# Batch 0 of an attention kernel: q and k transposed in quarters of 64 tokens by 64 channels

## The chip, the cores and the metric

The kernel runs on one core of a Trainium2 chip. The core has five engines with one instruction queue each: TensorE (PE in the profile, its weight loads PEld), VectorE (DVE), ScalarE (ACT), GpSimd (POOL) and SyncE (SP). Each engine works through its own queue in order, and waits at an instruction until the semaphores that it names have been raised. The metric is the device time of one execution in microseconds (us). Three executions of the kernel before took 171.11, 171.31 and 171.92 us; the median is 171.31 us.

## The reference

Four batches of eight attention heads, 768 tokens, 64 channels per head. A query sees itself and the 95 tokens before it, and the first 8 tokens of the sequence; the score gets a bias that falls with distance, by a slope of its own for each head. Then a second block works on the result x (768 tokens by 512 channels per batch).

```
scores = scale * q @ k.T + bias          # bias = -slope[h] * distance
a      = softmax(where(keep, scores, -1e9))
x      = a @ v                           # heads side by side: 768 x 512
theta  = x @ w_theta
y      = w_tok_r @ (x*cos(theta)) + w_tok_i @ (x*sin(theta))
u      = x + y
out    = u + relu(u @ w_ch)
```

## The kernel before

A token block is 128 tokens, so there are six blocks. Two heads are always worked together (h0 and h0+1): head h0 on partitions 0 to 63 of the transposed tiles, head h0+1 on partitions 64 to 127.

**Layout of q and k.** `load_qk` (L70) puts token 6p+t on partition p in column group t. The scores need q and k with channels on the partitions, so `att_transpose` (L209) turns them on TensorE into PSUM tiles of the pool `ps_tr` (two buffers), and copies bring them to one SBUF tile `qk`: its first 768 columns are `kT`, the next 768 `qT`, both with tokens in their natural order. Tokens of the first 64 partitions are tokens 0 to 383, tokens of the other 64 partitions are 384 to 767.

For batch 0 (L238 to L250) the function makes two PSUM tiles, `pq` and `pk`. It transposes 12 pieces of q (six column groups, two heads; 128 tokens by 64 channels each), then 12 of k. ScalarE then copies `pk` to `kT` and VectorE copies `pq` to `qT`; each copy takes 768 columns, or two cuts of 258 and 510 columns in the first call (`cuts=(43, T)`). For batches 1 to 3 (L216 to L237) it makes the two PSUM tiles `halves` by partition half instead: `halves[0]` holds k and q of tokens 0 to 383, `halves[1]` those of tokens 384 to 767. It takes 48 transposes of 64 tokens by 64 channels, and each of the two copies takes 768 columns that hold one half of kT and one half of qT.

**After the transposes.** `att_extras` (L254) copies kT's blocks 1 to 4 to a tile part `mT` (L257) and overwrites the first 8 tokens of each block there with the global tokens (L258); it does so on GpSimd, in the first call of batch 0 on VectorE. `prepare_v` (L91, L92) does the like for v. `att_scores` (L279) forms three groups of score blocks: group 0 works on kT alone, groups 1 and 2 need mT as well. In batch 0, groups 0 and 2 get their bias in PSUM from a matmul (`att_bias`, L276) and one exponential (L302); group 1 goes through an exponential (L306) and a multiplication with a table on VectorE (L319). `att_values` (L346) multiplies with v, `att_norm` (L362, L364) divides by the row sums on VectorE, and `turn_x` (L378, L383) transposes x for the next block.

**Order.** The whole order is written out by hand: `K` keeps every instruction in program order on its engine. Batch 0 runs ahead of everything else (L533 to L581):

```
    for h0 in (2, 4, 6):
        att_scores(0, h0, 0)
        att_scores(0, h0, 1, mul=False)
        att_values(0, h0 - 2, apart=True)
        att_norm(0, h0 - 2)
        att_norm(0, h0 - 1)
        if h0 < 6:
            att_transpose(0, h0 + 2)
            ...
        att_mul(0, h0, 1)
        att_scores(0, h0, 2)
```

So on TensorE the values of one pair of heads stand behind the group-1 scores of the next pair, and the transposes of the pair after stand behind those values; on VectorE the copy of a transposed half stands behind the four instructions of the two norms. In batches 1 to 3 the attention of one batch is interleaved with the second block of the batch before (`attend_beside`, L503). `keep_warm` (L133) puts matmuls on zeros into the TensorE queue, whose result nobody reads. The loads of batch 0's later heads, of the weights (`load_wtok`, L104) and of batch 1 stand in GpSimd's queue, between the copies of `att_extras` and `prepare_v`.

Of the kernel before, what the change touches and what calls it, by code (L numbers as in the profile page):

```python
# [16 lines left out]
def kernel(  # L17
# [13 lines left out]
    nc = tc.nc  # L31
    B, H, S, D = q.shape
    T = 128
    NT = S // T
# [19 lines left out]
    K = tc.keep_in_program_order  # L54
# [4 lines left out]
    def ps_acc():  # L59
        return psum.tile([T, DM], FP, name="ps_mm", tag="ps_mm", bufs=2)  # L60

    def ps_tr(cols):
        return psum.tile([T, cols], BF, name="ps_tr", tag="ps_tr", bufs=2)
# [4 lines left out]
    q_sb, k_sb, x_sb = {}, {}, {}  # L68
# [19 lines left out]
    def prepare_v(b, h0, eng=nc.gpsimd):  # L88
        hs = slice(h0, h0 + 2)
        vs, vp = v_sb[b % 2], v_pv[b % 2]  # L90
        K(eng.tensor_copy(out=vp[:, hs, :, :], in_=vs[:, hs, 1:NT - 1, :]))  # L91
        K(eng.tensor_copy(  # L92
            out=vp[0:NG, hs, :, :],
            in_=vs[0:NG, hs, 0:1, :].to_broadcast([NG, 2, NT - 2, D + 1])))
# [38 lines left out]
    def keep_warm(n, tile=None):  # L133

        junk = ps_acc() if tile is None else tile
        for _ in range(n):
            K(nc.tensor.matmul(junk, lhsT=zero[:, 0:T], rhs=zero, start=True, stop=True))
# [13 lines left out]
    ident = const.tile([T, T], BF)  # L151
# [54 lines left out]
    exps, probs, values = {}, {}, {}  # L206
    xTs, zris, css = {}, {}, {}

    def att_transpose(b, h0, extras=True, sins=None, q_eng="dve", between=None, cuts=(T,)):  # L209

        qk = abuf.tile([T, 2 * S + (NT - 2) * T], BF, name="qk", bufs=2)
        kT, qT = qk[:, 0:S], qk[:, S:2 * S]
        qTs[b, h0], kTs[b, h0] = qT, kT
        mTs[b, h0] = qk[:, 2 * S:]
        copy = nc.scalar.copy if q_eng == "act" else nc.vector.tensor_copy
        if b > 0:  # L216

            HP = T // 2
            halves = [ps_tr(S), ps_tr(S)]
            for t_ in range(NT):  # L220
                for i_, src in enumerate((k_sb[b], q_sb[b])):
                    c = (i_ * NT + t_) * HP
                    for r in range(2):
                        P = slice(r * HP, (r + 1) * HP)
                        for hh in range(2):
                            K(nc.tensor.transpose(  # L226
                                halves[r][hh * D:(hh + 1) * D, c:c + HP],
                                src[P, h0 + hh, t_ * D:(t_ + 1) * D], ident[P, P]))
            if sins is not None:
                sins()  # L230
            for r, op in enumerate((nc.scalar.copy, copy)):
                K(op(out=qk[:, 0:2 * S].rearrange("a (i r p t) -> a i r p t",  # L232
                                                  i=2, r=2, t=NT)[:, :, r, :, :],
                     in_=halves[r].rearrange("a (i t p) -> a i p t", i=2, t=NT)))
            if extras:
                att_extras(b, h0)
            return  # L237
        pq, pk = ps_tr(S), ps_tr(S)  # L238
        for src, pst in ((q_sb[b], pq), (k_sb[b], pk)):
            if pst is pk and between is not None:  # L240
                between()
            for t_ in range(NT):
                for hh in range(2):
                    K(nc.tensor.transpose(pst[hh * D:(hh + 1) * D, t_ * T:(t_ + 1) * T],
                                          src[:, h0 + hh, t_ * D:(t_ + 1) * D], ident))

        for op, dst, src in ((nc.scalar.copy, kT, pk), (copy, qT, pq)):
            for p0, p1 in zip((0,) + cuts, cuts):
                K(op(out=dst.rearrange("a (p t) -> a p t", t=NT)[:, p0:p1, :],  # L249
                     in_=src.rearrange("a (t p) -> a p t", t=NT)[:, p0:p1, :]))  # L250
        if extras:
            att_extras(b, h0)

    def att_extras(b, h0, eng=nc.gpsimd, values=True):  # L254
        kT = kTs[b, h0]
        mT = mTs[b, h0]
        K(eng.tensor_copy(out=mT, in_=kT[:, T:S - T]))  # L257
        K(eng.tensor_copy(  # L258
            out=mT.rearrange("a (t p) -> a t p", p=T)[:, :, 0:NG],
            in_=kT[:, None, 0:NG].to_broadcast([T, NT - 2, NG])))  # L260
        if eng is nc.gpsimd and values:
            prepare_v(b, h0)
# [3 lines left out]
    def att_bias(h0, g_):  # L266

        ps = biased[h0, g_] = ps_wide()
        rows = dist.rearrange("a n t -> a (n t)")
        for hh in range(2):  # L270
            if g_ == 0:
                out_, rhs = ps[:, hh, 0:3 * T], rows
            else:
                out_ = ps[:, hh, :].rearrange("a (r x) -> a r x", r=2)
                rhs = rows[:, None, T:3 * T].to_broadcast([T, 2, 2 * T])
            K(nc.tensor.matmul(out_, lhsT=ident_d[:, h0 + hh, :], rhs=rhs,  # L276
                               start=True, stop=False))

    def att_scores(b, h0, g_, mul=True):  # L279
        qT, kT, mT = qTs[b, h0], kTs[b, h0], mTs[b, h0]  # L280
        blocks = GROUPS[g_]
        n = len(blocks)
        bias = b == 0 and g_ != 1
        if bias and (h0, g_) not in biased:
            att_bias(h0, g_)
        ps = biased[h0, g_] if bias else ps_wide()

        runs = [(0, 2)] + [(2, 1)] if g_ == 0 else [(i_, 1) for i_ in range(n)]
        for i_, w in runs:
            it, prev = blocks[i_]  # L290
            if prev == 0 or it == 1:
                keys = kT[:, (it - prev) * T:(it - prev + 1) * T]
            else:
                keys = mT[:, (it - 2) * T:(it - 1) * T]
            for hh in range(2):
                R = slice(D * hh, D * (hh + 1))
                K(nc.tensor.matmul(ps[:, hh, i_ * T:(i_ + w) * T],  # L297
                                   lhsT=keys[R, :], rhs=qT[R, it * T:(it + w) * T],
                                   start=not bias, stop=not bias or i_ == n - 1))
        if bias:  # L300
            p = abuf.tile([T, 2, 4 * T], BF, name="p", bufs=6)
            K(nc.scalar.activation(p[:, :, 0:n * T], ps[:, :, 0:n * T], AF.Exp, scale=scale))  # L302
            probs[b, h0, g_] = p
            return
        e = abuf.tile([T, 2, 4 * T], BF, name="e", bufs=3)
        K(nc.scalar.activation(e[:, :, 0:n * T], ps[:, :, 0:n * T], AF.Exp, scale=scale))  # L306
        exps[b, h0, g_] = e
        if mul:
            att_mul(b, h0, g_)
# [193 lines left out]
    def attend_beside(b, main, lead, load):  # L503


        def m(n=1):
            for _ in range(n):
                main.pop(0)()

        m(lead)  # L510
        for h0 in range(0, H, 2):
            att_scores(b, h0, 0)
            m(2 if h0 else 1)
            att_scores(b, h0, 1)
            att_scores(b, h0, 2)
            if h0 + 2 < H:
                att_transpose(b, h0 + 2, q_eng="act")
                if load and h0 == 0:
                    load_heads(b + 1, 0, 4)
                if load and h0 + 4 == H:  # L520
                    load_heads(b + 1, 4, 4)
                m(2)
            else:
                if load:
                    turn_x(b, NC - 2, False)
                m(len(main) - 1)
            att_values(b, h0)
            if h0 + 2 < H and not (load and h0 + 4 == H):
                turn_x(b, h0 // 2, True)
        m()  # L530
# [4 lines left out]
    for src, dst in ((first[:, 0], q_sb[0]), (first[:, 1], k_sb[0])):  # L535
        K(nc.vector.tensor_copy(out=dst[:, 0:2, :], in_=src))
    att_bias(0, 0)
    att_transpose(0, 0, extras=False, between=lambda: keep_warm(1), cuts=(43, T))
    make_ident_d(2, 6)
    att_extras(0, 0, nc.vector)  # L540
    prepare_v(0, 0, nc.vector)
    keep_warm(1)
    att_scores(0, 0, 0)
    att_scores(0, 0, 1)
    att_transpose(0, 2, extras=False)
    att_extras(0, 2, nc.gpsimd, False)
    prepare_v(0, 2)
    load_wtok(0)
# [1 line left out]
# [4 lines that stand above are left out]
        att_norm(0, h0 - 2)  # L554
        att_norm(0, h0 - 1)
        if h0 < 6:
            att_transpose(0, h0 + 2)
            if h0 == 2:
                load_wtok(1)
            else:  # L560
                load_heads(1, 0, 4)
# [3 lines that stand above are left out]
            turn_x(0, h0 // 2 - 1, False)  # L565
# [101 lines left out]
```

## Time and profile before

| | |
|---|---|
| profiled execution, own time | 171.33 us |
| its span, first to last instruction | 169.5 us |
| median of three executions | 171.31 us |
| PE busy | 158.7 us (94% of the span), 1965 instructions |
| DVE busy | 114.7 us (68%) |
| ACT busy | 103.0 us (61%) |
| POOL busy | 63.2 us (37%) |
| transposes of batch 0 (L244) | 96, from 5.9 to 18.2 us |
| copies of batch 0 (L249) | 5 on VectorE, 5 on ScalarE, from 6.6 to 19.6 us |
| granted TensorE clock | 1.000 |

Times in the trace count from the start of the span. The busy shares are averages over a kernel with different stages: the first 36 us are batch 0 alone, in which the engines hand work to each other in turn, and after that TensorE has work of two batches at once. What a change in batch 0 is worth must therefore be read in the first 22 us. The chain of waits goes back from the last instruction: at each step it names what released it, or the instruction ahead of it on its engine.

### The profile page before, as it was taken

The numbers are of one execution on the slowest core, as the hardware profiler recorded it, in microseconds if no ns is written. First come the engines' busy times: TensorE is split into PE (matmuls) and PEld (weight loads), VectorE is DVE, ScalarE is ACT, GpSimd is POOL, SyncE is SP. The second block draws the span as 40 slices with busy tenths as digits, with TensorE's granted clock in tenths as the row PEclk, the third lists the DMA queues.
The fourth block names the chain that finished last, engine by engine and source line by source line (L and its number), as shares of the span: only waits on it lengthen the run. The fifth ranks groups of instructions, "written<-read, shape, count | busy, mean of one in ns | idle before, by whom it ended". The sixth has DMA issues, their size and how long they took to land.

```text
span 169.5 us, 4624 instructions
## 1 busy us (share of the span) xinstructions
PE 158.7 (94%) x1965; PEld 86.2 (51%) x1988; DVE 114.7 (68%) x210; ACT 103.0 (61%) x120; POOL 63.2 (37%) x99
## 2 busy tenths in 40 slices
PE   7779999999899999999999999999999999999992
PEld 2346665555465654446555554445655544444440
DVE  7768875965858875767587694849568756534362
ACT  4989887957686562798658615996765618300010
POOL 8996797004484650032972900054245000000000
PEclk9999999999999999999999999999999999999999
DMA  4999999999999999910599999711953342121325
GB/s 148 194 180 190 209 211 208 198 180 182 158 140 196 141 173 215 257 70 4 92 145 170 155 187 197 210 62 37 73 110 95 99 148 86 68 60 34 113 102 186
DMA packets 57060, 24.08 MB, mean 142 GB/s; under 512 B 43088, under 2 KB 54096, under 8 KB 57040
## 3 DMA queue, kind: packets, MB, share of 16 engines
q0 software_dynamic: 35328, 12.45, 65.5%
q1 hardware_dynamic: 21440, 10.95, 31.2%
q10 hardware_dynamic: 272, 0.39, 0.7%
q8 instruction: 15, 0.25, 0.6%
q14 instruction: 5, 0.04, 0.1%
HBM read 25.69 MB, written 6.29 MB: 189 GB/s over the span
## 4 chain that ended last, share of the span: by engine, by line
PE 80%; DVE 6%; DMA 4%; issue 3%; POOL 3%; ACT 3%; DVEq 0%; ACTq 0%; POOLq 0%
PE ps_mm L430 35%; PE ps_mm L472 12%; PE ps_w L395 11%; PE ps_w L297 7%; PE ps_w L346 5%; DMA v_sb<-in_v_dram 4%; PE ps_tr L226 3%; PE ps_mm L346 2%; ACT e L306 2%; PE ps_tr L114 2%; DVE zri L411 1%; DVE w_tokT L117 1%; PE ps_tr L378 1%; DVE p L319 1%; ACT qk L249 1%
## 5 line engine op out<-in xcount | busy, mean ns | idle before, releaser
L430 PE MATMUL ps_mm<-zri,w_tokT 128*128 128x512 bf16 x276 | 67.0, 380 | 1.3 <-issue 0.8
L306 ACT ACTIVATE e<-ps_w 128x1024 bf16<-128x1024 f32 (+1 forms) x40 | 37.1, 958 | 17.8 <-PE ps_w L297 17.8
L430 PEld LDWEIGHTS <-w_tokT 128*128 128x128 bf16 x288 | 26.2, 98 | 30.3 <-issue 2.3
L257 POOL COPY qk<-qk 128x512 bf16<-128x512 bf16 x15 | 9.5, 636 | 65.2 <-ACT qk L232 53.0
L319 DVE TENSOR_TENSOR p<-e,wmask 128x1024 bf16<-128x1024 bf16 x28 | 19.9, 712 | 11.8 <-ACT e L306 11.8
L403 ACT ACTIVATE cs<-ps_w,halfpi 128x1024 bf16<-128x1024 f32 x12 | 13.4, 1116 | 18.6 <-PE ps_w L395 18.6
L435 DVE TENSOR_TENSOR u<-x_sb,ps_mm 128x512 bf16<-128x512 bf16 x24 | 16.2, 683 | 12.2 <-PE ps_mm L430 12.2
L395 PE MATMUL ps_w<-w_theta_bf,xT 128*128 128x512 bf16 x91 | 22.6, 379 | 0.6 <-ACT cs L404 0.3
L411 DVE TENSOR_TENSOR zri<-cs,x_sb 128x1024 bf16<-128x1024 bf16 x24 | 16.1, 688 | 9.1 <-ACT cs L403 7.7
L472 PE MATMUL ps_mm<-w_ch_bf,uTd 128*128 128x512 bf16 x82 | 21.5, 379 | 0.6 <-issue 0.5
L297 PE MATMUL ps_w<-qk 64*128 64x128 bf16 (+1 forms) x320 | 16.1, 223 | 2.3 <-DVE qk L249 0.8
L475 DVE SCALAR_TENSOR_TENSOR o_sb<-ps_mm,u 128x512 f32<-128x512 f32 (+2 forms) x25 | 16.5, 664 | 1.1 <-PE ps_mm L472 0.9
L232 ACT COPY qk<-ps_tr 128x768 bf16<-128x768 bf16 x21 | 16.0, 815 | 2.0 <-issue 2.0
L297 PEld LDWEIGHTS <-qk 64*128 64x128 bf16 x320 | 10.0, 94 | 12.1 <-issue 7.8
L346 PEld LDWEIGHTS <-p 128*128 128x128 bf16 x352 | 13.2, 97 | 4.6 <-DVE p L319 0.8
L395 PEld LDWEIGHTS <-xT 128*128 128x128 bf16 x96 | 9.0, 98 | 10.8 <-issue 0.5
L80 POOL DMA_DIRECT2D v_sb<-in_v_dram x10 | 13.0, 1299 | 0.0
L472 PEld LDWEIGHTS <-uTd 128*128 128x128 bf16 x88 | 8.2, 98 | 9.0 <-issue 0.2
L404 ACT ACTIVATE cs<-ps_w 128x1024 bf16<-128x1024 f32 x12 | 12.2, 1020 | 0.0
L92 POOL COPY v_pv<-v_sb 8x520 bf16<-8x520 bf16 x15 | 11.5, 767 | 0.9
L354 DVE TENSOR_TENSOR x_sb<-ps_w,rec 128x768 bf16<-128x768 f32 x12 | 11.5, 958 | 0.4
L346 PE MATMUL ps_w<-v_sb,p 128*128 128x65 bf16 x168 | 11.3, 193 | 0.0
(84 smaller groups left out, 180.2 us busy)
## 6 DMA issues: line engine op xcount, KB each, us to landing
out_dram<-o_sb SPq DMA_DIRECT2D x23, 256.0 KB, 2.3
q_sb<-in_q_dram POOLq DMA_DIRECT2D x6, 384.0 KB, 6.2
k_sb<-in_k_dram POOLq DMA_DIRECT2D x6, 384.0 KB, 9.0
v_sb<-in_v_dram POOLq DMA_DIRECT2D x6, 384.0 KB, 13.5
w_nat<-in_moe_w_tok_r_dram POOLq DMA_DIRECT2D x1, 1152.0 KB, 12.3
w_nat<-in_moe_w_tok_i_dram POOLq DMA_DIRECT2D x1, 1152.0 KB, 13.4
v_sb<-in_v_dram POOLq DMA_DIRECT2D x4, 192.0 KB, 6.7
q_sb<-in_q_dram POOLq DMA_DIRECT2D x3, 192.0 KB, 5.9
```

Source lines behind the costliest of these rows:

```text
L232: K(op(out=qk[:, 0:2 * S].rearrange("a (i r p t) -> a i r p t", i=2, r=2, t=NT)[:, :, r, :, :], in_=halves[r].rearrange("a (i t p) -> a i ...
L297: K(nc.tensor.matmul(ps[:, hh, i_ * T:(i_ + w) * T], lhsT=keys[R, :], rhs=qT[R, it * T:(it + w) * T], start=not bias, stop=not bias or i_ ...
L306: K(nc.scalar.activation(e[:, :, 0:n * T], ps[:, :, 0:n * T], AF.Exp, scale=scale))
L319: K(nc.vector.tensor_mul(p.rearrange("a h (r x) -> a h r x", r=2), e.rearrange("a h (r x) -> a h r x", r=2), wmask[:, hs, None, T:3 * T].t ...
L346: K(nc.tensor.matmul(dst, lhsT=lhsT, rhs=rhs, start=(i_ == 0), stop=(i_ == len(mms) - 1)))
L395: K(nc.tensor.matmul(pth[:, s2, :], lhsT=xTs[b][:, dc, c:c + T], rhs=w_theta_bf[:, dc, :], start=(dc == 0), stop=(dc == NC - 1)))
L403: K(nc.scalar.activation(cs[:, :, 0, :], pth, AF.Sin, bias=halfpi))
L411: K(nc.vector.tensor_mul(zris[b][:, st:st + 2, wi, :].rearrange("a s (c d) -> a s c d", d=T), cs[:, :, wi, :].rearrange("a s (c d) -> a s ...
L430: K(nc.tensor.matmul(acc, lhsT=w_tokT[wi][:, st, tt * T:(tt + 1) * T], rhs=zris[b][:, st, wi, :], start=(done[b, tt] == 0), stop=(done[b, ...
L435: K(nc.vector.tensor_add(us[b][:, tt, :].rearrange("a (c d) -> a c d", d=T), x_sb[b][:, :, tt, :], acc.rearrange("a (c d) -> a c d", d=T)))
L472: K(nc.tensor.matmul(pc[:, 0:N], lhsT=uT[:, c:c + T], rhs=w_ch_bf[:, dc, cols], start=(dc == 0), stop=(dc == NC - 1)))
L475: K(nc.vector.scalar_tensor_tensor(o_sb, in0=pc[:, 0:N], scalar=0.0, in1=us[b][:, tt, cols], op0=ALU.max, op1=ALU.add))
```

## The change

Batch 0 takes the way of the other batches: two PSUM tiles by partition half, 48 transposes of 64 by 64, and two copies that each hold one half of k and q. The two ways become one function body, and a parameter `engs` names the engine of each of the two copies. In batch 0 VectorE copies the first half of the tokens and ScalarE the second. The first call transposes q before k (with one `keep_warm` matmul in between, as before) and no longer cuts its copies. Its `att_extras` now stands ahead of the six `make_ident_d` instructions on VectorE, and two more `keep_warm` matmuls stand between the group-0 and group-1 scores of the first pair of heads. For batches 1 to 3 the instructions and their order stay as they were; GpSimd's and SyncE's queues hold the same instructions in the same order throughout.

```diff
-    def att_transpose(b, h0, extras=True, sins=None, q_eng="dve", between=None, cuts=(T,)):
+    def att_transpose(b, h0, extras=True, sins=None, engs=("act", "dve"), between=None):
...
-        pq, pk = ps_tr(S), ps_tr(S)
-        for src, pst in ((q_sb[b], pq), (k_sb[b], pk)):
-            if pst is pk and between is not None:
+        HP = T // 2
+        halves = [ps_tr(S), ps_tr(S)]
+        order = [(t_, i_) for t_ in range(NT) for i_ in range(2)]
+        if between is not None:
+            order = [(t_, i_) for i_ in (1, 0) for t_ in range(NT)]
+        for n_, (t_, i_) in enumerate(order):
+            if n_ == NT and between is not None:
                 between()
-            for t_ in range(NT):
+            src = (k_sb[b], q_sb[b])[i_]
+            c = (i_ * NT + t_) * HP
+            for r in range(2):
+                P = slice(r * HP, (r + 1) * HP)
                 for hh in range(2):
-                    K(nc.tensor.transpose(pst[hh * D:(hh + 1) * D, t_ * T:(t_ + 1) * T],
-                                          src[:, h0 + hh, t_ * D:(t_ + 1) * D], ident))
-
-        for op, dst, src in ((nc.scalar.copy, kT, pk), (copy, qT, pq)):
-            for p0, p1 in zip((0,) + cuts, cuts):
-                K(op(out=dst.rearrange("a (p t) -> a p t", t=NT)[:, p0:p1, :],
-                     in_=src.rearrange("a (t p) -> a p t", t=NT)[:, p0:p1, :]))
+                    K(nc.tensor.transpose(halves[r][hh * D:(hh + 1) * D, c:c + HP],
+                                          src[P, h0 + hh, t_ * D:(t_ + 1) * D], ident[P, P]))
+        if sins is not None:
+            sins()
+
+        for r, eng in enumerate(engs):
+            K((nc.scalar.copy if eng == "act" else nc.vector.tensor_copy)(
+                out=qk[:, 0:2 * S].rearrange("a (i r p t) -> a i r p t",
+                                             i=2, r=2, t=NT)[:, :, r, :, :],
+                in_=halves[r].rearrange("a (i t p) -> a i p t", i=2, t=NT)))
...
-                att_transpose(b, h0 + 2, q_eng="act")
+                att_transpose(b, h0 + 2, engs=("act", "act"))
...
-    att_transpose(0, 0, extras=False, between=lambda: keep_warm(1), cuts=(43, T))
+    att_transpose(0, 0, extras=False, engs=("dve", "act"), between=lambda: keep_warm(1))
+    att_extras(0, 0, nc.vector)
     make_ident_d(2, 6)
-    att_extras(0, 0, nc.vector)
     prepare_v(0, 0, nc.vector)
     keep_warm(1)
     att_scores(0, 0, 0)
+    keep_warm(2)
     att_scores(0, 0, 1)
-    att_transpose(0, 2, extras=False)
+    att_transpose(0, 2, extras=False, engs=("dve", "act"))
...
-            att_transpose(0, h0 + 2)
+            att_transpose(0, h0 + 2, engs=("dve", "act"))
```

More of the change, by code (lines that the diff above doesn't have):

```diff
@@ L214, in att_transpose @@
         mTs[b, h0] = qk[:, 2 * S:]
[L215 to L219, printed above, removed]
-            for t_ in range(NT):
[L221 to L237, printed above, removed]
@@ L238, in att_transpose @@
-        pq, pk = ps_tr(S), ps_tr(S)
-        for src, pst in ((q_sb[b], pq), (k_sb[b], pk)):
-            if pst is pk and between is not None:
+        HP = T // 2
[5 more added lines that the diff above has]
+            if n_ == NT and between is not None:
                 between()
-            for t_ in range(NT):
+            src = (k_sb[b], q_sb[b])[i_]
+            c = (i_ * NT + t_) * HP
+            for r in range(2):
+                P = slice(r * HP, (r + 1) * HP)
```

## The prediction

> **What bounds the kernel now.** I read the page's shares first, then the chain of waits over the first 24 us, then the timeline of single engines there.
>
> ```profile
> span 169.5 us, 4624 instructions
> PE 80%; DVE 6%; DMA 4%; issue 3%; POOL 3%; ACT 3%; DVEq 0%; ACTq 0%; POOLq 0%
> ```
>
> TensorE carries 80% of the chain, but nearly all of it after 21 us. The changed lines run before that, where the chain of waits reads (start us, us, what):
>
> ```profile
> 3.03 6.30 DMA v_sb<-in_v_dram
> ...
> 9.35 0.92 DVE v_pv L91
> ...
> 11.18 0.88 DVE qk L249
> 12.06 0.04 issue
> 12.10 0.56 PE ps_w L297 x12
> 12.66 0.78 PE ps_mm L346 x22
> 13.44 0.77 PE ps_tr L244 x23
> 14.21 0.11 issue
> 14.32 0.81 ACT qk L249
> 15.13 0.05 issue
> 15.19 0.62 POOL qk L257
> 15.81 0.05 issue
> 15.86 0.56 POOL qk L258
> ```
>
> It goes on in the same circle: scores and values on PE, transposes, ScalarE's copy of k, GpSimd's two copies to mT, the next group-1 scores at 16.47, and once more until 20.75. Two things are to be seen. Until 9.33 us the kernel waits for the first load of v, which the change does not touch, so nothing gained before that counts. And in the circle it is ScalarE's copy, which now holds all of kT, that releases GpSimd. VectorE's copy of q is not on the chain there. Its timeline shows why that matters:
>
> ```profile
> 13.85 0.18 DVE L362 RECIPROCAL rec<-ps_mm 128x6 f32<-128x6 f32 x1
> 14.07 0.56 DVE L364 TENSOR_TENSOR x_sb<-ps_mm,rec 128x384 bf16<-128x384 f32 x1
> 14.54 0.95 DVE L249 COPY qk<-ps_tr 128x768 bf16<-128x768 bf16 x1
> 15.41 0.93 DVE L319 TENSOR_TENSOR p<-e,wmask 128x1024 bf16<-128x1024 bf16 x1
> ```
>
> The copy of q stands behind the norm of the second head and ends at 15.49, 0.36 us after ScalarE's copy of k (15.13). Nobody minds, since GpSimd needs only kT. After the change each copy holds half of kT, so L257 must wait for both; in the order of the built programs GpSimd's copy waits for ScalarE before, and for VectorE and ScalarE after.
>
> **The change part by part.**
>
> *Transposes.* 24 per call become 48. The same form runs in batches 1 to 3: 48 of them go from 36.45 to 37.03, 0.58 us, against 0.86 us for 24 of the old form (13.37 to 14.23). So they end 0.28 us earlier. In the two calls of the circle this buys nothing, as VectorE's copy starts later than they end (below). The next matmul then follows a gap of 0.16 us (37.03 to 37.19); start to next matmul is 0.74 us against 0.79 (13.37 to 14.16), so no cost.
>
> *Copies.* The new form has rows of its own: 951 to 957 ns on VectorE and 805 ns on ScalarE (L232), against 945 and 797 (L249, uncut). Below 0.02 us a call, taken as 0.
>
> *First call.* Before, the uncut parts start early: VectorE at 6.58, ScalarE at 7.36. After, both copies wait for all 48. The k part starts behind q's and the junk matmul, which was at 6.79; 24 quarters take about 0.19 us of issue and 0.20 of the last one's length, so the copies start at about 7.2 (estimate). Bounds: not before the cast of k ends (6.33) plus 0.39, 6.75, and not after the old end of the k part, 7.36. VectorE then has its copy 0.95, L257 0.30, L258 0.17 (its rows of before), about 0.07 of gaps, and six identity scalings 0.89, in this order: 2.38 us, to 9.57. The v copy L91 starts there instead of at 9.35: +0.2 (bounds 0, if it still waits for v, and +0.4). What follows, L92, L319 and the copy of the second call, moves along. ScalarE does not hold it: scores at 8.2 plus 0.34, exponentials 0.81 and 1.02 end at about 10.4, and L319 would start at 10.7.
>
> *The two extra junk matmuls.* They run at 0.21 us each (four of L430 take 0.86), while PE waited 0.69 us for VectorE's L258. Cost 0. Without that cover they would cost 0.43 us on PE, but the second exponential would still wait for the first (L302, 0.81), so less on the chain.
>
> *Second call (heads 2 and 3).* VectorE's copy ended at 12.06, ScalarE's at 10.97, and GpSimd started at 11.03 in between, so that mT was ready at 11.93, before VectorE's copy. Now mT comes behind it: 12.06 + 0.05 + 0.62 + 0.05 + 0.21 = 12.99, the scores of group 1 start 0.05 later and take 0.40, and the values start at 13.44 instead of 12.66: +0.78. In PE's queue the values, the transposes and the next scores all stand behind that wait.
>
> *Third and fourth call (the circle).* From the end of the values to the end of VectorE's copy it takes 2.05 us (13.44 to 15.49; 17.64 to 19.69), and these are norms and the copy, which the faster transposes do not shorten: they end 0.58 us after the values, the norms 1.19 us. GpSimd starts 0.06 us behind: 2.11 us after the values instead of 1.75 (13.44 to 15.19) and 1.83 (17.64 to 19.47). So +0.36 and +0.28. GpSimd's pair takes 1.23 us from start to end in both (15.19 to 16.42, 19.47 to 20.70), of which L258's 0.55 is long against 0.21 in most rows. I keep 1.23, since the same multiplication L319 runs beside it. Bounds: 0.62 + 0.05 + 0.21 = 0.88, which would take 0.35 off each call, and the multiplication ahead of GpSimd, +0.14 each (worked below).
>
> On that contention the row is L319: 0.93 and 1.02 us beside GpSimd's copies against a median of 0.69, with L258 stretched to 0.55; the two take turns. The Trainium skill, SBUF — State Buffer, section "SBUF: two separate sides", says that the port pair that VectorE and GpSimd share is an exclusive lock held for a whole instruction, and that whoever starts first blocks the other. By these rows the trace agrees, and after the change VectorE would start first; the rival below prices that.
>
> *Moved with it.* GpSimd's loads stand behind its copies and move by 1.0 to 1.6 us. The token weights (L102) go out at 13.12 and 17.60 and take 12.3 and 13.4 us: landed at 25.4 and 31.0, used at 27.67 and 33.08, and their users move by the same amount. Batch 1's q, k and v are used from 36.4 us on. Cost 0; the cover is about 2 us. From 21 us on the chain is PE, VectorE and ScalarE work with no transfer in it, so a delay at 20.75 goes through to the end.
>
> *Sum:* 0.2 + 0.78 + 0.36 + 0.28 = +1.62 us. The profiled execution took 171.33 us (span 169.5 and 1.8 around it), 0.02 above the median. 171.33 + 1.62 = 172.95 us.
>
> **The rivals.**
>
> 1. *The multiplication goes first and GpSimd waits.* In the third and fourth call GpSimd now starts 0.06 us after VectorE's copy ends, and L319 starts at that end or 0.08 us ahead of it, as the rows 14.54 + 0.95 and 15.41 show. Then L257 waits for it: 16.20 + 0.67 = 16.87, + 0.62 + 0.05 + 0.21 = 17.75 instead of 17.61. Twice 0.14: 173.2 us. Against it: L257 in the trace is never above 0.77 us, but it has hardly ever started just behind such an instruction. Still slower.
>
> 2. *GpSimd's pair gets shorter.* If L257 and L258 run undisturbed in 0.88 us, 0.7 us come back: 172.25 us. For it: 13 of 15 L258 take 0.21 us. Against it: both long rows stand beside exactly this multiplication.
>
> 3. *The delay is absorbed (no change).* If some link after 21 us waited in truth for a load that does not move, the 1.62 us would vanish in that wait: 171.3 us. The place would be the first matmuls on w_theta (22.68) or the transposes of the token weights (27.67, 33.08). It decides when such a load lands less than 1.62 us ahead of its use. Against it: w_theta, sent at 10.12 with 9.7 us to landing, is there at 19.8, and the token weights' loads move along with their users.
>
> 4. *VectorE is not late (not slower).* If VectorE were free whenever the transposes end, its copy of the second call would be done before ScalarE's (10.97), which costs nothing, and in the circle GpSimd would be released 0.58 + 0.04 + 0.95 + 0.05 = 1.62 us after the values instead of 1.75 and 1.83: 0.34 us gained, 171.0 us. It decides where the copy of the third call starts, in old times: before 14.19 it gains, behind it loses. The last norm occupies VectorE until 14.63, and VectorE keeps its written order, so the trace speaks against it.
>
> **How the numbers follow.** Main forecast 172.95: 0.58. Rival 1: 0.16. Rival 2: 0.11. Rival 3: 0.09. Rival 4: 0.06, half of it with the shorter pair of rival 2 on top, which makes it 170.3. A difference of 0.5%, 0.86 us, is about what a measurement of this kernel can tell from no change: slower means above 172.17, faster below 170.45. The main case and rival 1 are slower, and rival 2 in 8 parts of 11: slower 0.82. Faster is the half of rival 4: 0.03. Same is the rest: 0.15. The main case's own range has the first call at 0 to 0.4 and half of the contention's bounds: 172.5 to 173.5. The range down to 171.9 takes in rival 2 with the first call at 0 (171.33 + 0.7 = 172.05), and up to 174.0 rival 1 with the first call at 0.4 and one more blocked GpSimd copy (0.34).
>
> **What the profile after will show.** L245 (the old L257) on GpSimd released by VectorE's copy and not ScalarE's, starting near 12.3, 16.5 and 21.1 us. ScalarE's copy done 0.6 us or more before VectorE's. PE idle ahead of the group-1 scores of heads 2, 4 and 6. Transposes of a call within 0.6 us. The first batch-1 transposes near 38.1 instead of 36.45. The forecast is wrong if VectorE's copy starts when the transposes end, if GpSimd starts before it is done, or if the batch-1 transposes start near 36.5.

## The result, and the profile after

The changed kernel is slower. Its median is 173.46 us (172.95 to 173.71, six executions); the kernel before, run beside it, had 171.42 us (171.11 to 171.92, six executions). The ratio is 1.0114, with a 95% interval of 1.0093 to 1.0135: 1.6 to 2.3 us. The ratios here and below are of fast executions alone and can differ by up to 0.2% from the quotient of the medians beside them. The profiled execution took 173.48 us. The page opens:

```profile
span 171.7 us, 4845 instructions
PE 76%; DVE 9%; DMA 7%; issue 2%; POOL 2%; ACT 2%; DVEq 0%; POOLq 0%; ACTq 0%
```

VectorE's part of the chain has gone from 6% to 9%, and DMA's from 4% to 7%. Both are read below. This is the chain of waits over batch 0 in the changed kernel (start us, us, what):

```profile
8.16 0.85 PE ps_mm L137 x2
9.01 0.56 PE ps_w L285 x7
...
9.60 1.03 ACT e L294
...
10.65 0.69 DVE p L307
11.34 0.88 DVE qk L235
...
12.36 0.62 POOL qk L245
...
13.04 0.22 POOL qk L246
...
13.30 0.40 PE ps_w L285 x8
13.70 0.46 PE ps_mm L334 x11
...
15.66 0.88 DVE qk L235
...
16.66 0.94 POOL qk L245
...
17.65 0.22 POOL qk L246
...
17.92 0.40 PE ps_w L285 x8
```

Before, TensorE went on from VectorE's second-call copy straight to the scores at 12.10 and the values at 12.66. GpSimd's two copies of that call started behind ScalarE's copy and were done ahead of VectorE's, as its timeline before shows:

```profile
11.03 0.63 POOL L257 COPY qk<-qk 128x512 bf16<-128x512 bf16 x1
11.72 0.21 POOL L258 COPY qk<-qk 128x32 bf16<-128x32 bf16 x1
```

Now GpSimd's two copies (L245 and L246, the old L257 and L258) stand between VectorE's copy and the group-1 scores: from 12.22 to 13.30. In the circle, ScalarE's copy has left the chain. The norms and VectorE's copy (15.66) have taken its place, and GpSimd starts behind them. The timelines of GpSimd (with the releaser in brackets) and of VectorE, in the changed kernel, say the same:

```profile
12.36 0.61 POOL L245 COPY qk<-qk 128x512 bf16<-128x512 bf16 x1 [1.44 <-DVE qk L235]
16.66 0.94 POOL L245 COPY qk<-qk 128x512 bf16<-128x512 bf16 x1 [1.40 <-DVE qk L235]
```

and on VectorE the multiplication that starts ahead of the second of them:

```profile
16.44 0.68 DVE L307 TENSOR_TENSOR p<-e,wmask 128x1024 bf16<-128x1024 bf16 x1
```

ScalarE's copies end at 11.31, 15.92 and 20.62 in its own timeline, 0.91, 0.62 and 0.54 us before VectorE's (12.22, 16.54, 21.16).

The same instructions in both profiles give the delay step by step:

| instruction | before | after | shift | added by this step |
|---|---|---|---|---|
| first multiplication (VectorE) | 10.51 | 10.65 | +0.14 | 0.14 |
| end of VectorE's second-call copy | 12.06 | 12.22 | +0.16 | 0.02 |
| values of heads 0 and 1 start | 12.66 | 13.70 | +1.04 | 0.88 |
| group-1 scores of heads 4, 5 | 16.47 | 17.92 | +1.45 | 0.41 |
| group-1 scores of heads 6, 7 | 20.75 | 22.54 | +1.79 | 0.34 |
| first transposes of batch 1 | 36.52 | 38.32 | +1.80 | 0.01 |
| TensorE's work from 106 us on | | | +2.18 | 0.38 |

From 27 to 103 us the shift stays at 1.80, so nothing on the way absorbs what batch 0 has lost. The last 0.38 us is not batch 0. In the chain of waits of the changed kernel it stands here:

```profile
96.84 8.33 DMA uTd<-u
...
105.21 1.04 PE ps_mm L460 x4
```

This load transposes a tile of `u`. Before, it went out at 95.05, took 7.7 us and landed at 102.76, only 0.07 us before TensorE began to load it as weights (102.83); TensorE did not wait. Now it takes 8.33 us, and TensorE waits. In the two chains its user starts 2.00 us later than before (105.21 and 103.21), and the four matmuls take 1.04 instead of 0.86 us. With the first load of q and k (4.25 us, now at the head of the chain where the load of v was with 6.30) this 8.33 us makes DMA's 7%.

One more thing differs. The windows view of the changed kernel (stretch, length, busy us of PE, PEld, DVE, ACT, POOL with instruction counts, granted TensorE clock, DMA share, GB/s) reads:

```profile
9.00:10.20 1.20, 1.20 (x57) 1.00 (x56) 1.09 (x4) 0.62 (x2) 1.20 (x3) 0.50 1.60 165
...
12.00:14.00 2.00, 1.29 (x26) 0.71 (x25) 0.21 (x1) 1.85 (x3) 1.51 (x4) 1.00 1.75 186
```

For about 3.4 us, from 8.3 to 11.7, TensorE ran at half its clock; the kernel before ran at 1.00 throughout. The six executions speak against a large price: two had the full clock all through and took 172.95 and 173.66 us, the four with a low stretch 173.42 to 173.71. Still, a second theory had to be tested: that the low clock, not the later link to GpSimd, makes the loss.

### The profile page after: what moved, and what is told of

It reads as the page before. It is cut to its first block, busy times and chain, and to the rows that moved or that the text cites. A ratio compares the mean times of both kernels' runs of the same rounds, so it can differ in the third digit from the quotient of the medians.

```text
span 171.7 us, 4845 instructions
## 1 busy us (share of the span) xinstructions
PE 161.5 (94%) x2086; PEld 85.5 (50%) x2086; DVE 114.3 (67%) x209; ACT 103.0 (60%) x119; POOL 63.1 (37%) x99
## 3 DMA queue, kind: packets, MB, share of 16 engines
q0 software_dynamic: 35328, 12.45, 67.6%
## 4 chain that ended last, share of the span: by engine, by line
PE 76%; DVE 9%; DMA 7%; issue 2%; POOL 2%; ACT 2%; DVEq 0%; POOLq 0%; ACTq 0%
PE ps_mm L418 34%; PE ps_mm L460 11%; PE ps_w L383 10%; PE ps_w L285 7%; PE ps_w L334 5%; DMA uTd<-u 5%; PE ps_tr L229 4%; DMA first<-in_q_dram 2%; DVE qk L235 2%; DVE w_tokT L117 2%; ACT e L294 2%; POOL qk L245 1%; PE ps_tr L114 1%; DVE zri L399 1%; PE ps_mm L334 1%
## 5 line engine op out<-in xcount | busy, mean ns | idle before, releaser
L418 PE MATMUL ps_mm<-zri,w_tokT 128*128 128x512 bf16 x288 | 68.7, 380 | 0.1
L245 POOL COPY qk<-qk 128x512 bf16<-128x512 bf16 x15 | 10.2, 678 | 67.4 <-ACT qk L235 53.4
L307 DVE TENSOR_TENSOR p<-e,wmask 128x1024 bf16<-128x1024 bf16 x28 | 19.4, 691 | 12.2 <-ACT e L294 12.2
L391 ACT ACTIVATE cs<-ps_w,halfpi 128x1024 bf16<-128x1024 f32 x12 | 13.4, 1116 | 19.0 <-PE ps_w L383 18.9
L460 PE MATMUL ps_mm<-w_ch_bf,uTd 128*128 128x512 bf16 x88 | 22.5, 379 | 0.2 <-DMA uTd<-u 0.2
L235 ACT COPY qk<-ps_tr 128x768 bf16<-128x768 bf16 x25 | 19.1, 811 | 2.8 <-issue 2.0
L285 PE MATMUL ps_w<-qk 64*128 64x128 bf16 (+1 forms) x320 | 16.6, 227 | 3.4 <-POOL qk L246 2.3
L463 DVE SCALAR_TENSOR_TENSOR o_sb<-ps_mm,u 128x512 f32<-128x512 f32 (+2 forms) x25 | 16.5, 664 | 1.1 <-PE ps_mm L460 0.9
L92 POOL COPY v_pv<-v_sb 8x520 bf16<-8x520 bf16 x15 | 11.5, 765 | 0.9
## 6 DMA issues: line engine op xcount, KB each, us to landing
v_sb<-in_v_dram POOLq DMA_DIRECT2D x6, 384.0 KB, 14.1
```

The lines of the kernel that those rows point to most:

```text
L235: K((nc.scalar.copy if eng == "act" else nc.vector.tensor_copy)(out=qk[:, 0:2 * S].rearrange("a (i r p t) -> a i r p t", i=2, r=2, t=NT)[: ...
L285: K(nc.tensor.matmul(ps[:, hh, i_ * T:(i_ + w) * T], lhsT=keys[R, :], rhs=qT[R, it * T:(it + w) * T], start=not bias, stop=not bias or i_ ...
L307: K(nc.vector.tensor_mul(p.rearrange("a h (r x) -> a h r x", r=2), e.rearrange("a h (r x) -> a h r x", r=2), wmask[:, hs, None, T:3 * T].t ...
L391: K(nc.scalar.activation(cs[:, :, 0, :], pth, AF.Sin, bias=halfpi))
L418: K(nc.tensor.matmul(acc, lhsT=w_tokT[wi][:, st, tt * T:(tt + 1) * T], rhs=zris[b][:, st, wi, :], start=(done[b, tt] == 0), stop=(done[b, ...
L460: K(nc.tensor.matmul(pc[:, 0:N], lhsT=uT[:, c:c + T], rhs=w_ch_bf[:, dc, cols], start=(dc == 0), stop=(dc == NC - 1)))
```

## The experiments

Theory A, from the prediction: each copy now holds half of kT, so GpSimd waits for VectorE, which is late, and every link to GpSimd passes its lateness on to the end. Theory B: small transposes or the lower clock on TensorE cost the time. Each "before" below is the kernel before on the same chip in the same runs. "Batch-1 shift" is the shift of the same instructions between 27 and 103 us against the profile of the kernel before. It leaves out the wait for `uTd` near 105 us, which turned up in the profiles with 0 to 1.6 us and is in the times.

For kernels built on the one before, `att_transpose` got a parameter `half`, which takes the changed kernel's transposes and copies; only the calls are shown.

### Small transposes, but whole k and whole q per engine

The changed kernel, with 48 transposes as it has them. In batch 0 ScalarE copies k's two halves and VectorE q's, in copies of 384 columns.

```diff
+        if b == 0:
+            HS = S // 2
+            for i_, op in ((0, nc.scalar.copy), (1, nc.vector.tensor_copy)):
+                for r in range(2):
+                    K(op(out=qk[:, i_ * S + r * HS:i_ * S + (r + 1) * HS].rearrange(
+                            "a (p t) -> a p t", t=NT),
+                         in_=halves[r][:, i_ * HS:(i_ + 1) * HS].rearrange(
+                            "a (t p) -> a p t", t=NT)))
+            if extras:
+                att_extras(b, h0)
+            return
```

> The change as it is, with one thing undone in batch 0: from the two half tiles ScalarE now copies both halves of k (two copies of 384 columns) and VectorE both halves of q, so that GpSimd's L257 no longer waits for VectorE. Theory (GpSimd waits for VectorE's late copy): the circle shortens from 2.2 us between values and GpSimd to about 0.58 + 0.04 + 0.95 + 0.05 = 1.62, below the 1.75 and 1.83 of the kernel before; the second call costs 0.2 to 0.4, since ScalarE's copies then end near 11.5 and not at 12.2; 171.2 to 171.9 us. Rival A (the 48 small transposes, their mode change or the low clock of 9 to 12 us cost the time): 173.2 to 173.6, as all of that stays.

Measured: 172.17 against 171.33 us, ratio 1.0048 (1.0032 to 1.0064), batch-1 shift +0.36 to +0.40. The clock was 1.00 in the profile. Its chain of waits:

```profile
12.49 0.75 PE ps_w L297 x12
13.24 0.78 PE ps_mm L346 x22
...
17.06 0.40 PE ps_w L297 x8
...
21.09 0.40 PE ps_w L297 x8
```

The link from VectorE's copy to GpSimd is gone, and the scores follow VectorE's copy again (it ends at 12.45). More than half of the loss goes with it, though the time lies above the range expected, since the circle got no shorter than before. In the circle, values to group-1 scores takes 3.82 us (13.24 to 17.06) against 3.81 before (12.66 to 16.47), and the next circle 4.03 against 4.28. What is left arises in the first call and the second: VectorE's copy there ends at 12.45 instead of 12.06 and the values start 0.58 us late, of which the last circle gives 0.25 back. The 48 small transposes alone are no loss in the circle.

### One call at a time

The second call alone:

```diff
-    att_transpose(0, 2, extras=False)
+    att_transpose(0, 2, extras=False, half=True)
```

> The kernel before, with the new way in the second call alone (heads 2 and 3). Theory: GpSimd starts behind VectorE's copy, 12.3 instead of 11.03, and the values 0.78 to 0.9 later: +0.8 to +0.9 us, 172.2 to 172.3. Rival A: under +0.3 us, as the transposes of one call are off the chain there.

Measured: 174.88 against 171.33 us, ratio 1.0209 (1.0173 to 1.0245), batch-1 shift +1.67. That is worse than the whole change, and a miss. The chain of waits has two parts:

```profile
13.33 0.78 PE ps_mm L352 x22
14.11 1.39 PE ps_tr L250 x24
15.50 0.97 PE ps_w L282 x2
```

The values start at 13.33, +0.67, the loss that theory A gives this call. Then the granted clock falls to 0.50 from 14.1 to 17.5 us: the 24 old transposes take 1.39 us instead of 0.81, and the two bias matmuls behind them 0.97 instead of 0.54 (14.16 to the next start at 14.70 before). That is the other 1.0 us. Five of its six executions show a lower mean clock; the sixth, at full clock, took 173.93 us, and its span is 171.6 us against 172.5 in the profile. The profile also holds 1.31 us of waiting for `uTd`.

The third and fourth call alone:

```diff
-            att_transpose(0, h0 + 2)
+            att_transpose(0, h0 + 2, half=True)
```

> The kernel before, with the new way in the third and fourth call alone. Theory: 0.3 to 0.4 us for each, +0.6 to +0.8 us, 172.0 to 172.2. Rival A: these two calls would carry about half of the loss, +0.9 to +1.0, and GpSimd would start no later behind the values than before.

Measured: 172.77 against 171.33 us, ratio 1.0068 (1.0023 to 1.0113), batch-1 shift +1.04 at full clock. Of this, 0.19 us was there before the first changed instruction (values at 12.85 instead of 12.66). The chain:

```profile
15.81 0.94 POOL qk L263
...
16.80 0.22 POOL qk L264
...
17.07 0.40 PE ps_w L303 x8
...
21.78 0.40 PE ps_w L303 x8
```

Group-1 scores at 17.07 and 21.78 instead of 16.47 and 20.75: +0.41 and +0.43 of its own. Theory A had +0.36 and +0.28. The time is above the range expected; the 0.19 and a wait of 0.40 for `uTd` are in it.

The first call alone, with the order of VectorE's instructions and the two matmuls on zeros that go with it:

```diff
-    att_transpose(0, 0, extras=False, between=lambda: keep_warm(1), cuts=(43, T))
-    make_ident_d(2, 6)
+    att_transpose(0, 0, extras=False, between=lambda: keep_warm(1), half=True)
     att_extras(0, 0, nc.vector)
+    make_ident_d(2, 6)
     prepare_v(0, 0, nc.vector)
     keep_warm(1)
     att_scores(0, 0, 0)
+    keep_warm(2)
     att_scores(0, 0, 1)
```

> The kernel before, with the new way in the first call alone, its order and its two extra junk matmuls included. Theory: +0.1 to +0.3 us, 171.5 to 171.7, since the first multiplication of VectorE moves from 10.51 to 10.65 in the two traces. Rival B (the clock, which falls to half between 8.2 and 11.7 us in the trace of after, carries the loss): +0.8 us or more, and the low clock appears here too.

Measured: 172.77 against 171.33 us, ratio 1.0085 (1.0060 to 1.0110), batch-1 shift +0.43, no stretch of half clock, and 1.58 us of waiting for `uTd` in the profile. The batch-0 part is larger than the +0.16 that the whole change lost there. The first multiplication starts at 10.94 instead of 10.51. VectorE's six identity scalings take 1.36 us instead of 0.89, but that costs nothing: the first copy of v (L91) ends at 10.30, against 10.26 before. The second copy of v (L92) makes the loss, with 0.68 us (10.33 to 11.01) instead of 0.28 (10.29 to 10.58). Both copies run beside GpSimd's issuing of loads. By the rows in the last section VectorE's copies end late beside such an issue, and a few hundredths of a us decide whether L92 is hit. So this call's price varies from kernel to kernel between about 0 (below) and 0.4.

The three parts' batch-1 losses, +0.43, +0.67 (at full clock) and +0.84, add up to 1.94; the whole has 1.80.

### All but the second call

The `half` way in the first, third and fourth call, with the order and the two matmuls on zeros that go with the first; the second call as before.

```diff
-    att_transpose(0, 0, extras=False, between=lambda: keep_warm(1), cuts=(43, T))
+    att_transpose(0, 0, extras=False, between=lambda: keep_warm(1), half=True)
...
-            att_transpose(0, h0 + 2)
+            att_transpose(0, h0 + 2, half=True)
```

> The new way in the first, third and fourth call, the old one in the second. Theory (the second call costs 0.87 in the traces with full clock, beside the others): 172.4 to 172.7 us. Rival (the parts do not add, since the low clock of TensorE picks another stretch whenever the order changes): 173.2 us or more, with a low clock in the trace.

Measured: 172.19 against 171.93 us, ratio 1.0014 (0.9992 to 1.0035), batch-1 shift +0.77. The time does not differ from before in these runs, which is better than expected; the trace shows the circle's loss all the same, with values at 12.70 and group-1 scores at 16.91 and 21.53. The two are not of one baseline: the shift counts from a profile of 171.33 us, and the kernel before had a median of 171.93 in these runs. Against the changed kernel's +1.80, the second call carries 1.03 us, the largest single part.

### The low clock taken away

First the two added matmuls on zeros are left out, which leaves the computation as it is:

```diff
     att_scores(0, 0, 0)
-    keep_warm(2)
     att_scores(0, 0, 1)
```

> The changed kernel without its two extra junk matmuls between the group-0 and group-1 scores. In its trace they took 0.85 us of the chain at half clock (8.16 to 9.01). Theory C (they lie on the chain, as the clock is low there): the group-1 scores of the first pair start at about 8.45 instead of 9.01 and the first multiplication 0.3 to 0.4 us earlier, 173.0 to 173.2 us. Rival (they hold the clock up for what follows): without them the low clock lasts longer or moves into the circle, 173.6 to 174.5 us.

Measured: 173.32 against 171.66 us, ratio 1.0103 (1.0065 to 1.0142), batch-1 shift +2.15. The half clock does not go; it moves, to 13.0 to 16.5 us. One of the six executions had the full clock and took 172.62 us, the others 173.04 to 174.44. In this profile the load of v also landed later, at 9.98 us, so it does not isolate what the two matmuls cost.

Then four matmuls on zeros instead of one behind the first transposes:

```diff
     prepare_v(0, 0, nc.vector)
-    keep_warm(1)
+    keep_warm(4)
     att_scores(0, 0, 0)
```

> The changed kernel with four junk matmuls instead of one behind the first call's transposes, in the stretch from 7.1 to 7.8 us in which TensorE waits for VectorE's copy. Theory C (the idle stretch is what lowers the clock at 8.2): the clock stays at 1.00 through 12 us, and the first pair gains 0.3 to 0.4 us, 173.0 to 173.2 us. Rival (the clock has no part in the result): unchanged, 173.4 to 173.5.

Measured: 173.69 against 171.66 us, ratio 1.0120 (1.0087 to 1.0152), batch-1 shift +1.61. The profiled execution had the full clock throughout and took 173.60 us. Of its other five, one more had it (173.55); the four with a low stretch took 173.51 to 173.94. The chain at full clock:

```profile
11.18 0.88 DVE qk L235
...
12.20 0.62 POOL qk L245
...
13.13 0.40 PE ps_w L285 x8
13.53 0.46 PE ps_mm L334 x11
...
17.75 0.40 PE ps_w L285 x8
...
22.36 0.40 PE ps_w L285 x8
```

VectorE's copy stands where it stood before (11.18), so the first call costs nothing here. The loss that remains is theory A alone: values at 13.53 (+0.87), group-1 scores at 17.75 (+1.28, so +0.41) and 22.36 (+1.61, so +0.33). The time stayed above the range that theory C gave. Theory B falls as the main cause: the time is lost with the clock at 1.00, too.

### Only GpSimd made late

The kernel before, transposes and copies untouched. GpSimd does its first copy to mT twice in the second to fourth call; the output is the same.

```diff
         mT = mTs[b, h0]
+        if b == 0 and h0 > 0:
+            K(eng.tensor_copy(out=mT, in_=kT[:, T:S - T]))
         K(eng.tensor_copy(out=mT, in_=kT[:, T:S - T]))
```

> The kernel before, transposes and copies untouched, but GpSimd makes its first copy to mT twice in the second, third and fourth call, so that mT comes 0.62 + 0.05 us later. Theory (GpSimd's lateness alone carries the loss): second call +0.35 (mT at 12.60 instead of 11.93, where the scores stand at 12.27), third and fourth +0.6 to +0.7 each; batch 1's first transposes 1.5 to 1.8 us later, 172.9 to 173.3 us. Rival (the chain has slack there, and the loss comes from the transposes, the copies' split or the clock): under +0.5 us.

Measured: 173.77 against 171.93 us, ratio 1.0114 (1.0084 to 1.0143), batch-1 shift +1.85, clock 1.00 in the profile. The chain:

```profile
13.16 0.78 PE ps_mm L348 x22
...
15.69 0.62 POOL qk L258
...
16.36 0.96 POOL qk L259
...
17.38 0.22 POOL qk L260
...
17.64 0.40 PE ps_w L299 x8
...
22.59 0.40 PE ps_w L299 x8
```

One extra copy and its gap are 0.67 us (15.69 to 16.36). The group-1 scores move by 0.67 more in each circle (17.64 is +1.17, 22.59 is +1.84), and by less in the second call (values +0.50), where GpSimd's end had some slack ahead of VectorE's copy. The 1.84 us goes through to the batch-1 shift, 1.85. The time is 0.5 us above the range expected, the shift just above its 1.5 to 1.8. This is the change's ratio without one changed transpose: a late end of GpSimd's pair is enough.

### Can the link be hidden?

If VectorE is late because its norms come first, the transposes and copies could stand ahead of the values and norms. In both kernels the same lines move (in the changed one shown, and so in the one before):

```diff
         att_scores(0, h0, 1, mul=False)
-        att_values(0, h0 - 2, apart=True)
-        att_norm(0, h0 - 2)
-        att_norm(0, h0 - 1)
         if h0 < 6:
             att_transpose(0, h0 + 2, engs=("dve", "act"))
...
+        att_values(0, h0 - 2, apart=True)
+        att_norm(0, h0 - 2)
+        att_norm(0, h0 - 1)
         att_mul(0, h0, 1)
```

> The changed kernel, with the transposes and copies of the third and fourth call put ahead of the values and norms of the pair before, so that VectorE's copy no longer stands behind the norms. Theory (the copy's place behind the norms sets GpSimd's start): GpSimd starts about 1.7 us after the group-1 scores instead of 2.9, the circle is then bound by the norms and the transposes of x at about 4.1 us instead of 4.6, 172.3 to 172.7 us. Rival (GpSimd's and VectorE's contention or the small transposes set the circle): 4.5 us or more per circle, 173.2 to 173.6.

Measured: 173.36 against 171.66 us, ratio 1.0099 (1.0063 to 1.0135), batch-1 shift +1.89, with half clock from 13.4 to 16.8 us in the profile. The first circle, 13.13 to 18.11 between group-1 scores, falls in that stretch. Two of its six executions had the full clock, with 173.30 and 172.59 us, against 173.55 and 173.60 in the full-clock run above; that is too few to tell whether the order pays.

> The kernel before with the same move: transposes and copies ahead of the values and norms. Theory: the circle falls from 4.28 to about 4.0 us, where TensorE's and ScalarE's own work and the transposes of x bound it, 170.7 to 171.1 us. Rival (the chain of waits misnames the circle): unchanged, 171.3 to 171.5.

Measured: 171.97 against 171.66 us, ratio 1.0013 (0.9989 to 1.0037), batch-1 shift +0.64 up to 68 us, where a wait of 0.82 us for `uTd` comes on top. No gain. Of the 0.64 us, 0.42 is there before the first moved line: the second copy of v takes 0.71 us instead of 0.28, as in the first-call kernel. In its chain ScalarE's exponential comes ahead of its copy, and VectorE's next copy ends up behind GpSimd's copies of v:

```profile
13.92 0.70 ACT e L306
14.62 0.70 ACT qk L249
...
17.22 0.62 POOL v_pv L92
...
17.89 0.96 DVE qk L249
```

In the changed kernel, with only the norms behind the copy on VectorE:

```diff
         att_values(0, h0 - 2, apart=True)
-        att_norm(0, h0 - 2)
-        att_norm(0, h0 - 1)
         if h0 < 6:
...
+        att_norm(0, h0 - 2)
+        att_norm(0, h0 - 1)
         att_mul(0, h0, 1)
```

> The changed kernel with the four instructions of the two norms behind the transposes' copy on VectorE instead of ahead of it, in the third and fourth call. Theory: VectorE's copy starts when the transposes end, and GpSimd about 1.75 us after the end of the values instead of 2.2; but the transposes of x now wait for the late norms and stand ahead of the group-1 scores on TensorE, so most of it is lost again: 173.2 to 173.5 us, and 0 to 0.2 us less per circle. Rival (GpSimd's start is set by something other than VectorE's queue): GpSimd starts 2.2 us after the values as before.

Measured: 175.46 against 171.93 us, ratio 1.0212 (1.0183 to 1.0242), batch-1 shift +3.17, much worse than expected. The chain:

```profile
14.73 0.57 PE ps_tr L229 x48
15.30 0.94 DVE qk L235
...
17.69 0.51 PE ps_tr L366 x6
...
18.52 0.49 PE ps_w L285 x12
```

VectorE's copy does start when the transposes end (15.30), as wanted. But the transposes of x (L366) need the norms and stand ahead of the next scores on TensorE, so the scores wait for norms that now end at 17.64. The circle grows to 5.1 us (values 13.95 to 19.02). This profile also has half clock from 8.2 to 11.6 us, the second copy of v at 0.72 us, and 1.23 us of waiting for `uTd`.

Last, the kernel before with small transposes in the third and fourth call alone, k copied by ScalarE and q by VectorE as in the first experiment:

```diff
-            att_transpose(0, h0 + 2)
+            att_transpose(0, h0 + 2, half=True)
```

> The kernel before, with the third and fourth call by small transposes, both halves of k copied by ScalarE and both halves of q by VectorE. In the trace of the first experiment the two circles took 3.82 and 4.03 us against 3.81 and 4.28 before: theory -0.1 to -0.3 us, 171.1 to 171.4 us, which could be too little to measure. Rival (small transposes cost in themselves): +0.4 us or more.

Measured: 172.99 against 171.93 us, ratio 1.0072 (1.0037 to 1.0106), a miss; batch-1 shift +0.46 to +0.50, and 0.60 us of waiting for `uTd`. The third call gained 0.12 us (16.35 against 16.47). The fourth lost it again:

```profile
16.35 0.40 PE ps_w L313 x8
...
17.52 0.18 PE ps_tr L231 x5
17.70 0.54 issue
18.24 0.59 PE ps_tr L231 x43
```

TensorE stops for 0.54 us inside the 48 transposes. What it waits for there was not settled. No version beat the kernel before.

## Why the prediction was right

The direction, the time (172.95 forecast, 173.46 measured) and the mechanism held, and the main case came out rather than a rival. Term by term, with the shift table and the full-clock run (four matmuls on zeros):

- *First call, +0.2.* +0.16 in the changed kernel, 0.00 in the full-clock run, +0.43 with this call alone. That the changed kernel came near it is luck, as three steps of it failed. The copies started at 6.81, not 7.2. The 0.92 us of the v copy L91, which the sum moved along as it was, is not its own length: it took 0.30 at 9.24 in the changed kernel, and before it ran until 10.26 beside GpSimd's issuing of a load (last section), so not the load of v alone set its end. And ScalarE, forecast to be done at about 10.4, did hold the multiplication: its second exponential ended at 10.63, since TensorE's scores for it (9.01 to 9.57) stood behind the junk matmuls (L137) at half clock.
- *The two junk matmuls, 0.* Their duration was mis-sized. They were costed at 0.21 us each and took 0.43 at half clock, in the chain: the forecast cover of 0.69 us did not hold them. In the full-clock run the second exponential starts at 9.21 with them, and at 9.25 before without them, so there the 0 held. The run without them cannot give their price, since the low clock moved.
- *Second call, +0.78.* +0.88 and +0.87 (+0.67 with this call alone, where VectorE's copy ended 0.21 us earlier than before). In the first two the missing 0.1 is GpSimd's start: 0.14 us behind VectorE's copy (12.22 to 12.36), where the sum had 0.05. The kernel before had a row for it, in the first call of batch 1, whose halves are copied by two engines: VectorE's copy ends at 38.15 and GpSimd's starts at 38.28.
- *Third and fourth call, +0.36 and +0.28.* +0.41 and +0.34. Again the start, 0.12 us behind (16.54 to 16.66) instead of 0.06. In the built program L245 now waits for two engines.
- *GpSimd's pair, 1.23 us.* 1.21 (16.66 to 17.87). The size held by luck, since the forecast kept it for the old order, and the inner split did not: L245 takes 0.94 and L246 0.22, where before it was 0.62 and 0.56. The multiplication starts first, at 16.44, and runs its undisturbed 0.68. That is the order of rival 1, but without its price: fully held back, L245 would start at 17.12 and end at 17.73 by its undisturbed 0.61; it ends at 17.60. The Trainium skill, SBUF — State Buffer, section "SBUF: two separate sides", has the first starter keep the shared port pair for its whole instruction. The trace agrees in that the first starter is unharmed and the second stretched by 0.33 us, and leaves 0.13 us less blocking than rival 1 made of it.
- *Rival 2 (a shorter pair)* fell with that row. *Rival 3 (absorbed)* fell with the constant 1.80 from 27 to 103 us. *Rival 4 (VectorE not late)* fell with the chain, where the norms lead without a gap to VectorE's copy; ScalarE's was done 0.54 to 0.91 us earlier.
- *Not in the sum:* the wait for `uTd`, +0.38 in the profile. The forecast read that no transfer was in the chain after 21 us and took that for slack. The load was there only 0.07 us before its use. It took 7.2 to 7.8 us in the three profiles without this wait (the kernel before and two experiments) and 8.1 to 9.5 in the eleven with a wait of 0.2 to 1.6 us, on both kernels' bases. Whether the change or the run sets its length is open.
- *The signs.* GpSimd's starts (12.36, 16.66 and 21.28) and its releaser came as forecast. Two signs were missed by a little: in the fourth call ScalarE's copy was 0.54 us ahead, not 0.6, and the second call's transposes took 0.86 us at half clock (9.48 to 10.34), not 0.6.

The sum of the terms to 103 us was 1.62, and 1.80 came; the profiled time differs by 2.15, the other 0.35 being the transfer and rounding. The medians differ by 2.04.

## What to carry to other kernels

When work is split between two engines, ask what the next engine needs: a split by operand lets it start after the one copy it needs, a split by halves makes it wait for the later of the two. Look for the later one in the timeline of the engine that is not in the chain; here VectorE's copies ended 1.09, 0.36 and 0.28 us behind ScalarE's, unseen, and the change turned that into 0.88, 0.41 and 0.34 us. And a transfer that does not show in the chain is not thereby early: compare its landing with its use.

## What the runs showed of the hardware

- *The granted clock falls without TensorE standing idle, and changes only at fixed steps.* In each of the 14 traces it changes at whole multiples of 3.41 us from its rise to full (4.84, 8.26 and 11.67 in the changed kernel), and a low stretch in batch 0 is one such step at 0.50. What goes with a drop is TensorE's work in the step ahead, counted by these steps. Up to 1.80 us of work, the next step was low each time: 1.68 without the junk matmuls (9.63 to 13.04), 1.71 with the transposes moved ahead in the changed kernel (9.92 to 13.34), 1.80 in the second-call kernel (10.71 to 14.12). With 2.27 us or more it was never low; the kernel before has 2.58 and 2.62 in its first two steps. Between these both occur: 2.19 in the changed kernel (4.84 to 8.26) led to a drop, 2.00 in the full-clock run (9.32 to 12.73) did not. So an edit of a few instructions moves or removes the drop, and the rise that the steps count from differs too (3.88 to 7.12 us). The Trainium skill, TensorE: Matmul & The Clock Gate, section "Part 1: The HAM clock gate (the "warmup" mystery)", has half rate after an idle window of about 3.4 us whose phase does not follow the kernel; the length, the half rate and the phase agree, while no 3.4 us ahead of these drops were idle.
- *A low stretch costs where TensorE is in the chain.* It cost about 1.0 us in the second-call kernel (14.1 to 17.5) and little in the changed one (8.3 to 11.7), where the first multiplication came 0.14 us late and the chain from 9.60 on runs over ScalarE and VectorE.
- *GpSimd starts 0.12 to 0.14 us behind the copy that releases it when it waits for VectorE and ScalarE*, against 0.05 to 0.06 behind ScalarE's alone in the kernel before. The chain of the changed kernel has a step of GpSimd's sequencer there (12.25, 0.02 us), which the waits for ScalarE alone do not have. Whether the second engine or VectorE as the releaser makes the difference, no run here separates.
- *VectorE's copies within SBUF end late beside GpSimd's issuing of a load.* The rows fit a hold from about 0.5 us after the start of the issue to 0.1 us behind its end; no run was made to test it. The first copy of v (L91) takes 0.30 us where it ends early in such an issue (9.24 to 9.54 in the changed kernel). In nine of the 14 profiles it starts between 9.35 and 9.79 and ends between 10.25 and 10.30, 0.11 to 0.15 us behind the end of the issue (10.13 to 10.17). So the load of v, which landed at 9.33 us before and between 9.28 and 9.98 in other profiles, rarely sets the end of this copy. The second copy of v, starting at 10.29 to 10.34, takes 0.28 us in seven profiles, where it would end 0.35 to 0.50 us into the issue of the next load, and 0.68 to 0.72 in three, where it would end 0.50 to 0.53 into it. That is the 0.4 us by which the first call's price varies.
